# Windowed attention with two gated layers on one core: which engines divide the attention weights, and when the first loads are taken to land

## The chip, the core and the metric

The kernel runs on one core of a Trainium2 chip. The metric is the device time of one execution in microseconds (us), as the median of several runs. The core has TensorE (PE, with its weight loads as PEld), VectorE (DVE), ScalarE (ACT), GpSimd (POOL) and SyncE (SP), which issues most of the loads and stores.

## What is computed

The input is q, k and v for 2 batches of 8 heads, 768 positions and 64 channels. Each position attends to the last 96 positions and to 8 global ones, with a bias that falls with distance. The result, 2 x 768 x 512, goes through two gated layers. All data are float32, the weights of the layers arrive in 64 bits.

```python
scores = scale * q @ k.T + bias            # masked to the window and the global keys
a = np.exp(scores - scores.max(-1))
a = a / (a.sum(-1) + 1e-9)                 # the division that the change moves
x = (a @ v) as 2 x 768 x 512
x = (sigmoid(causal_conv5(x)) * (x @ w_val)) @ w_out
h = relu(x @ w_in2)
out = (h * sigmoid(conv3(h))) @ w_out2
```

The kernel multiplies w_out and w_in2 into one matrix W first, so that the values of the first layer go straight to the hidden units of the second.

## The kernel before

Attention is done in 12 tiles of 128 queries, 6 for each batch (`fast_attention`). A tile needs the keys of itself and of the tile before. For each half of four heads PE writes the scores to PSUM (line 492). DVE adds the bias and takes the extreme of each row (line 503), ACT takes the exponential with its row sum (line 508), POOL adds 1e-9 to four sums (line 519), DVE takes the reciprocals (line 522), and then each of the four heads' weights, the tile `p`, is multiplied by its reciprocal. That last step is called a division here. It is done by DVE (line 529) or by POOL (line 532).

Then, for two heads at a time, PE transposes the weights into the PSUM tile `t` (line 559), ACT or DVE copies them to `pts` (lines 563 and 569), and PE multiplies them with the values into the PSUM tile `x` (line 584). The ring of `t` has a single buffer, so each transposition of two heads waits for the copy of the two before. The tile's result is moved to SBUF on line 601 (ACT) or 607 (DVE).

Meanwhile the weights of the layers are loaded in units of 128 rows and brought from 64 bits to float32 (`to_f32`: lines 272 on ACT, 274 on POOL, 279 and 282 on DVE). PE makes W of them (line 337). The first product of W needs five such units. `hidden_inputs`, `values` (lines 246, 253 to 255, 697, 698, 702, 755) and later `hidden` and `project` follow.

The order on each engine is made when the kernel is built. `Plan.add` takes each step with the engines that can do it and a cost in us for each. `Plan.lay` runs through the steps in a modelled time: the step goes to the engine where it would end first by these costs, from the times in `START` on. Steps of the loads issued ahead (`LANDED`) count as done at the given times. `Plan.issue` then writes every engine's instructions in that order, and each engine keeps to it. A cost or a time in these tables therefore changes no instruction by itself: it changes which engine does a step and where the step stands.

```python
here: ends = {o: max(free[o], est[w]) + us for o, (us, _) in w.ways.items()}
```

Of the kernel before, what the change touches and what calls it, by code (L numbers as in the profile page):

```python
# [13 lines left out]
AF = mybir.ActivationFunctionType  # L14
ALU = mybir.AluOpType
# [24 lines left out]
XPAIRS = 2  # L40
RAWS, MBUFS, HBUFS, Z2BUFS, PBUFS, PTBUFS, KQBUFS, VBUFS = 3, 2, 6, 3, 11, 4, 3, 4
EARLY = -5.0
LANDED = {("k", 1): 2.5, ("k", 2): 3.8, ("r", 1): 5.1, ("v", 1): 6.5, ("r", 2): 7.8}
LANDING = 2.4
ORDERED = {getattr(mybir.EngineType, e) for e in ("PE", "DVE", "Activation", "Pool")}
BANKS = {"s": 4, "t": 1, "x": 1, "f": 2}
# [38 lines left out]
class Plan:  # L85

    LAG = {"PE": 0.2, "ACT": 0.15, "DVE": 0.15, "POOL": 0.15, "SP": 0.0, "AHEAD": 0.0}
    START = {"DVE": 0.4, "ACT": 1.2, "SP": 4.9}  # L90
    SWITCH = 0.1
    STICK = 3.0
    PASSES = 6
# [127 lines left out]
def act_us(n, sbuf=True, scaled=False, sums=False):  # L221
    return 0.05 + 0.000834 * n + 0.042 * sbuf + 0.092 * scaled + 0.093 * sums
# [10 lines left out]
def pool_us(n):  # L233
    return 0.17 + 0.0013 * n
# [201 lines left out]
def fast_attention(c, ap):  # L436

    nc, ident, pl = c.nc, c.ident, c.plan
# [13 lines left out]
    def keys(t, pr, what):  # L452
        return key_tile(t)[:, pr, what]
# [21 lines left out]
    for t in range(nt):  # L475
        b, i = tiles[t]
        if t and i == 0:
            yield
        js = [t - 1, t] if i else [t]
        nk = len(js) * P  # L480
        st, p = sts.new(), {}
        load(t)
        for half in range(2):
            s = [c.ring["s"].new() for z in range(2)]

            def scores(half=half, s=s, js=js, t0=t):
                for pr in (2 * half, 2 * half + 1):
                    for n, j in enumerate(js):
                        for z in range(2):
                            hs = slice(z * D, (z + 1) * D)  # L490
                            out = s[z].t.rearrange("p (a w) -> p a w", w=WIN)[:, pr % 2, n * P : (n + 1) * P]
                            nc.tensor.matmul(out, keys(t0, pr, 1)[hs], keys(j, pr, 0)[hs], start=True, stop=True)  # L492

            pl.add(
                "PE", 0.43 * len(js), scores, s + held(kq, js), [("kq", j) for j in js], [("s", t, half)], mode="s"
            )
            for h in range(4 * half, 4 * half + 4):
                p[h] = pr_.new()

                def least(h=h, s=s, st=st, w=p[h], nk=nk, i=i):  # L500
                    sc = s[h % 2].t.rearrange("p (a w) -> p a w", w=WIN)[:, h // 2 % 2, :nk]
                    bias = c.B[:, h, :] if i else c.B0[h]
                    nc.vector.tensor_tensor_reduce(  # L503
                        w.t[:, :nk], sc, bias, -QKSCALE, 3.0e38, ALU.add, ALU.min, st.t[:, 0, h : h + 1]
                    )

                def grow(h=h, st=st, w=p[h], nk=nk):
                    nc.scalar.activation(  # L508
                        w.t[:, :nk], w.t[:, :nk], AF.Exp, bias=st.t[:, 0, h : h + 1], scale=-1.0,
                        accum_out=st.t[:, 1, h : h + 1],  # L510
                    )

                bias = ("B" if i else "B0", h)
                pl.add("DVE", dve_us(nk), least, [p[h], s[h % 2], st], [("s", t, half), bias], [("p", t, h)])
                pl.add("ACT", act_us(nk, True, True, True), grow, [p[h], st], [], [("p", t, h)])
            hs = slice(4 * half, 4 * half + 4)

            def guard(st=st, hs=hs):
                nc.gpsimd.tensor_scalar(st.t[:, 1, hs], st.t[:, 1, hs], 1.0e-9, 1.0, ALU.add, ALU.mult)

            def invert(st=st, hs=hs):
                nc.vector.reciprocal(st.t[:, 2, hs], st.t[:, 1, hs])  # L522

            four = [("p", t, h) for h in range(4 * half, 4 * half + 4)]
            pl.add("POOL", 0.12, guard, [st], four, [("r", t, half)])
            pl.add("DVE", 0.2, invert, [st], [], [("r", t, half)])
            for h in range(4 * half, 4 * half + 4):
                def on_dve(h=h, st=st, w=p[h], nk=nk):
                    nc.vector.tensor_scalar(w.t[:, :nk], w.t[:, :nk], st.t[:, 2, h : h + 1], None, ALU.mult)  # L529

                def on_pool(h=h, st=st, w=p[h], nk=nk):
                    nc.gpsimd.tensor_scalar(w.t[:, :nk], w.t[:, :nk], st.t[:, 2, h : h + 1], 1.0, ALU.mult, ALU.mult)  # L532

                pl.add(
                    "DVE", 0.13 + 0.00052 * nk, on_dve, [p[h], st], [("r", t, half)], [("p", t, h)],
                    POOL=(0.2 + pool_us(nk), on_pool),
                )

        def first_keys(t=t, i=i):
            r = key_tile(t)[:, :, 0, 0:GW]  # L540
            a, z = (gl, r) if i == 0 else (r, gl)
            nc.gpsimd.tensor_scalar(a, z, 1.0, 1.0, ALU.mult, ALU.mult)

        if i == 0:
            pl.add("POOL", 0.4, first_keys, held(kq, [t]), [("kq", t)], ["gl"])
        elif i < NT - 1:
            pl.add("POOL", 0.4, first_keys, held(kq, [t]), ["gl"], [("kq", t)])

        xp = c.ring["x"].new()
        pts = {}  # L550
        for pr in range(NPAIR):
            pt = c.ring["t"].new()
            pts[pr] = ptr.new()

            def turn(pr=pr, pt=pt, p=p, nw=len(js)):
                o = pt.t.rearrange("p (z n q) -> p z n q", z=2, n=2)
                for z in range(2):
                    for n in range(nw):
                        nc.tensor.transpose(o[:, z, n, :], p[2 * pr + z].t[:, n * P : (n + 1) * P], ident)  # L559

            def copy(pt=pt, w=pts[pr], nw=len(js)):
                o = pt.t.rearrange("p (z n q) -> p z n q", z=2, n=2)
                nc.scalar.activation(w.t[:, :, :nw, :], o[:, :, :nw, :], AF.Copy)  # L563

            two = [p[2 * pr], p[2 * pr + 1]]
            pl.add("PE", 0.218 * len(js), turn, [pt] + two, [("p", t, 2 * pr), ("p", t, 2 * pr + 1)], [("pt", t, pr)])
            def by_dve(pt=pt, w=pts[pr], nw=len(js)):
                o = pt.t.rearrange("p (z n q) -> p z n q", z=2, n=2)
                nc.vector.tensor_copy(w.t[:, :, :nw, :], o[:, :, :nw, :])

            pl.add(
                "ACT", act_us(2 * nk, False), copy, [pt, pts[pr]], [("pt", t, pr)], [("pts", t, pr)],
                DVE=(dve_us(2 * nk), by_dve),
            )

            if pr % XPAIRS < XPAIRS - 1:
                continue

            def output(prs=range(pr - XPAIRS + 1, pr + 1), pts=pts, xp=xp, js=js):
                o = xp.t.rearrange("p (a q) -> p a q", q=P)  # L580
                for pr in prs:
                    for n, j in enumerate(js):
                        for z in range(2):
                            nc.tensor.matmul(  # L584
                                o[z * D : (z + 1) * D, pr, :], vals(j, 2 * pr + z), pts[pr].t[:, z, n, :],
                                start=n == 0, stop=n == len(js) - 1,
                            )

            prs = range(pr - XPAIRS + 1, pr + 1)
            pl.add(  # L590
                "PE", 0.213 * len(js) * XPAIRS, output, [xp] + [pts[q] for q in prs] + held(vs, js),
                [("pts", t, q) for q in prs] + [("v", j) for j in js], [("xp", t, q) for q in prs], mode="x",
            )
        if 0 < i < NT - 1:
            pl.add(
                "SP", dma_us(64), lambda b=b, t=t: nc.sync.dma_start(vs[t].t[0:GW], c.v[b, 0:GW].rearrange("s (a h) d -> s a h d", a=2)),
                [vs[t]], [], [("v", t)], delay=LANDING,
            )
        pl.add(
            "ACT", act_us(512, False),  # L600
            lambda xp=xp, i=i: nc.scalar.activation(
                c.x[:, :, XP + i * P : XP + (i + 1) * P], xp.t.rearrange("p (a q) -> p a q", q=P), AF.Copy
            ),
            [xp], [("xp", t, pr) for pr in range(NPAIR)], [("x", i)] + (["d", "d0"] if t in (0, 1, 4) else []),
            DVE=(
                dve_us(512),
                lambda xp=xp, i=i: nc.vector.tensor_copy(
                    c.x[:, :, XP + i * P : XP + (i + 1) * P], xp.t.rearrange("p (a q) -> p a q", q=P)
                ),
            ),  # L610
        )
# [431 lines left out]
```

## Time and profile before

| | |
|---|---|
| median of 3 runs | 285.67 us (285.6 to 286.19) |
| the profiled execution | 285.83 us |
| its span, from first to last instruction | 284.0 us |
| busy PE | 268.7 us, 95% |
| busy DVE | 235.2 us, 83% |
| busy ACT | 190.2 us, 67% |
| busy POOL | 96.7 us, 34% |

The span is the profiled execution without what lies around it (1.8 us). The shares are means over stages that differ, so the stages have to be read one by one. The time of an instruction in the trace is longer than the distance at which two of them follow each other on an engine, since the end of one lies over the start of the next.

### The profile page before, as it was taken

How to read it: one execution, taken by the hardware profiler on the slowest of the kernel's cores; microseconds unless marked ns; L12 is line 12 of the kernel's file. 1: busy time of each engine (PE TensorE's matmuls, PEld its weight loads, DVE VectorE, ACT ScalarE, POOL GpSimd, SP SyncE). 2: the span in 40 equal slices, each digit the busy share in tenths (PEclk: the TensorE clock that was granted, in tenths of full speed). 3: DMA queues.
4: the chain of work that ended last, by engine and by line, in shares of the span. 5: the costliest groups of instructions: out<-in, count | busy, mean ns of one | idle time of the engine just before them, and what ended most of it. 6: DMA issues, size and time to landing. Idle time of an engine off the chain costs nothing.

```text
span 284.0 us, 5446 instructions
## 1 busy us (share of the span) xinstructions
PE 268.7 (95%) x1832; PEld 227.7 (80%) x1832; DVE 235.2 (83%) x599; ACT 190.2 (67%) x476; POOL 96.7 (34%) x207
## 2 busy tenths in 40 slices
PE   3979999999989989999999999999999999999993
PEld 2857746555569979999899999989999988899883
DVE  3999999999999999998999999999985554357600
ACT  2999984976798798797877455884474354444520
POOL 4544563662395536622446012130412000003000
PEclk9999999999999999999999999999999999999999
DMA  5995554854480320004400000010000020000121
GB/s 155 358 338 186 219 180 150 291 175 149 148 264 35 121 75 14 35 13 158 150 0 0 2 0 1 8 48 21 37 2 0 0 76 37 37 0 2 40 111 48
DMA packets 10421, 26.18 MB, mean 92 GB/s; under 512 B 1424, under 2 KB 2704, under 8 KB 10384
## 3 DMA queue, kind: packets, MB, share of 16 engines
q1 hardware_dynamic: 9968, 25.22, 26.2%
q10 hardware_dynamic: 416, 0.52, 0.5%
q8 instruction: 16, 0.26, 0.4%
q14 instruction: 21, 0.17, 0.2%
HBM read 22.59 MB, written 3.15 MB: 91 GB/s over the span
## 4 chain that ended last, share of the span: by engine, by line
PE 70%; DVE 21%; ACT 3%; issue 3%; POOL 2%; DVEq 1%; ACTq 0%; POOLq 0%
PE s L254 8%; PE s L255 8%; PE s L253 8%; PE f L255 5%; PE f L254 5%; PE f L253 5%; PE s L492 5%; DVE z L702 4%; PE t L559 4%; PE x L584 4%; DVE p L503 4%; PE f L337 4%; PE t L253 2%; DVE p L529 2%; PE x L255 2%
## 5 line engine op out<-in xcount | busy, mean ns | idle before, releaser
L702 DVE SCALAR_TENSOR_TENSOR z<-h,cw,z 128x384 f32<-128x384 f32 x64 | 39.9, 629 | 12.7 <-ACT z L697 10.9
L508 ACT ACTIVATE p<-p,st 128x256 f32<-128x256 f32 (+1 forms) x96 | 46.1, 483 | 6.4 <-DVE st L503 6.4
L704 ACT ACTIVATE z<-z 128x384 f32<-128x384 f32 (+2 forms) x48 | 25.1, 523 | 25.0 <-DVE z L702 24.6
L254 PE MATMUL s<-w,g 128*128 128x512 f32 (+1 forms) x104 | 39.2, 377 | 0.0
L255 PE MATMUL s<-w,g 128*128 128x512 f32 (+1 forms) x104 | 39.2, 377 | 0.0
L702 DVE SCALAR_TENSOR_TENSOR z<-x,cw,z 128x400 f32<-128x400 f32 (+1 forms) x64 | 39.1, 642 | 0.1
L253 PE MATMUL s<-w,g 128*128 128x512 f32 (+1 forms) x104 | 39.1, 376 | 0.0
L532 POOL TENSOR_SCALAR p<-p,st 128x256 f32<-128x256 f32 (+1 forms) x48 | 32.4, 683 | 11.3 <-DVE st L522 6.9
L559 PE MATMUL t<-ident,p 128*128 128x128 f32 x176 | 28.6, 281 | 5.6 <-ACT pts L563 3.4
L559 PEld LDWEIGHTS t<-ident,p 128*128 128x128 f32 x176 | 19.8, 141 | 15.6 <-ACT pts L563 5.9
L503 DVE CUSTOM_DVE_ANT_0 p<-s,B 128x256 f32<-128x256 f32 x80 | 30.8, 412 | 0.3 <-PE s L492 0.3
L337 PE MATMUL f<-w,w 128*128 128x512 f32 x64 | 29.8, 597 | 0.1
L253 PE MATMUL f<-gg,Wh 128*128 128x400 f32 (+1 forms) x80 | 27.7, 346 | 0.0
L255 PE MATMUL f<-gg,Wl 128*128 128x400 f32 (+1 forms) x80 | 27.0, 338 | 0.0
L254 PE MATMUL f<-gg,Wh 128*128 128x400 f32 (+1 forms) x80 | 27.0, 338 | 0.0
L563 ACT ACTIVATE pts<-t 128x512 f32<-128x512 f32 (+1 forms) x40 | 22.1, 552 | 5.7 <-PE t L559 3.7
L274 POOL TENSOR_SCALAR raw<-raw 128x512 f32<-128x512 f32 x24 | 18.1, 754 | 19.8 <-ACT m L272 12.5
L698 POOL TENSOR_SCALAR z<-h,cw 128x384 f32<-128x384 f32 x9 | 8.3, 923 | 44.5 <-DVE z L702 31.0
L246 DVE TENSOR_TENSOR g<-z,g 128x384 fp32r<-128x384 f32 x32 | 17.9, 567 | 5.9 <-ACT g L244 5.9
L255 PEld LDWEIGHTS s<-w,g 128*128 128x128 f32 x104 | 19.5, 188 | 3.9
L254 PEld LDWEIGHTS s<-w,g 128*128 128x128 f32 x104 | 19.5, 188 | 2.8
L253 PEld LDWEIGHTS s<-w,g 128*128 128x128 f32 x104 | 19.5, 188 | 2.8
(125 smaller groups left out, 657.3 us busy)
## 6 DMA issues: line engine op xcount, KB each, us to landing
raw<-in_moe_w_out_dram SPq DMA_DIRECT2D x12, 512.0 KB, 3.5
raw<-in_moe_w_in_dram SPq DMA_DIRECT2D x8, 512.0 KB, 5.2
k<-in_kq_dram SPq DMA_DIRECT2D x7, 512.0 KB, 4.9
v<-in_v_dram SPq DMA_DIRECT2D x11, 256.0 KB, 4.1
out_dram<-o SPq DMA_DIRECT2D x11, 256.0 KB, 2.0
raw<-in_moe_w_val_dram SPq DMA_DIRECT2D x4, 512.0 KB, 3.6
kq<-in_kq_dram SPq DMA_DIRECT2D x3, 512.0 KB, 4.7
v<-in_v_dram SPq DMA_DIRECT2D x8, 64.0 KB, 2.8
```

Source lines behind the costliest of these rows:

```text
L253: nc.tensor.matmul(out, lh, rh, start=first, stop=False)
L254: nc.tensor.matmul(out, lh, rl, start=False, stop=False)
L255: nc.tensor.matmul(out, ll, rh, start=False, stop=last)
L274: "POOL", pool_us(n), lambda: nc.gpsimd.tensor_scalar(whole(), whole(), 0.0, 1.0, ALU.mult, ALU.mult),
L337: nc.tensor.matmul(ps.t, big["wot"].t.bitcast(F32)[:, e, cs], big[wi].t.bitcast(F32)[:, e, :], start=e == 0, stop=e == 3)
L503: nc.vector.tensor_tensor_reduce(w.t[:, :nk], sc, bias, -QKSCALE, 3.0e38, ALU.add, ALU.min, st.t[:, 0, h : h + 1])
L508: nc.scalar.activation(w.t[:, :nk], w.t[:, :nk], AF.Exp, bias=st.t[:, 0, h : h + 1], scale=-1.0, accum_out=st.t[:, 1, h : h + 1],)
L532: nc.gpsimd.tensor_scalar(w.t[:, :nk], w.t[:, :nk], st.t[:, 2, h : h + 1], 1.0, ALU.mult, ALU.mult)
L559: nc.tensor.transpose(o[:, z, n, :], p[2 * pr + z].t[:, n * P : (n + 1) * P], ident)
L563: nc.scalar.activation(w.t[:, :, :nw, :], o[:, :, :nw, :], AF.Copy)
L702: nc.vector.scalar_tensor_tensor(z(), src(k), w()[:, k : k + 1], z(), ALU.mult, ALU.add)
L704: pl.add("ACT", act_us(n), lambda: nc.scalar.activation(z(), z(), AF.Tanh, scale=0.5), bufs, [], [token])
```

## The change

The division's second way is an ACTIVATE with the reciprocals as its scale on ACT, in place of a TENSOR_SCALAR on POOL. The modelled cost on DVE for 256 columns goes from 0.26 to 0.35. The modelled landings of five early loads and the time from which SP is free are later by 0.5 to 1.4 us. Nothing else is edited; the order on all engines is worked out anew.

```diff
-LANDED = {("k", 1): 2.5, ("k", 2): 3.8, ("r", 1): 5.1, ("v", 1): 6.5, ("r", 2): 7.8}
+LANDED = {("k", 1): 3.0, ("k", 2): 5.0, ("r", 1): 6.3, ("v", 1): 7.7, ("r", 2): 9.0}
...
-    START = {"DVE": 0.4, "ACT": 1.2, "SP": 4.9}
+    START = {"DVE": 0.4, "ACT": 1.2, "SP": 6.3}
...
-                def on_pool(h=h, st=st, w=p[h], nk=nk):
-                    nc.gpsimd.tensor_scalar(w.t[:, :nk], w.t[:, :nk], st.t[:, 2, h : h + 1], 1.0, ALU.mult, ALU.mult)
+                def on_act(h=h, st=st, w=p[h], nk=nk):
+                    nc.scalar.activation(w.t[:, :nk], w.t[:, :nk], AF.Copy, scale=st.t[:, 2, h : h + 1])
 
                 pl.add(
-                    "DVE", 0.13 + 0.00052 * nk, on_dve, [p[h], st], [("r", t, half)], [("p", t, h)],
-                    POOL=(0.2 + pool_us(nk), on_pool),
+                    "DVE", 0.22 + 0.00052 * nk, on_dve, [p[h], st], [("r", t, half)], [("p", t, h)],
+                    ACT=(act_us(nk, True, True), on_act),
                 )
```

Of the 96 divisions DVE has 48 and POOL 48 before; with the change DVE has 49, ACT 47 and POOL none. Of the 48 copies to `pts` DVE has 8 before and 14 with the change. ACT has two masks before (line 400) and one with the change, DVE three (line 401, 256 columns) and one, POOL three (line 399) and six.

The first place is PE at the start, after the scores of tile 1 (`k_71` and `k_72` are the keys of tiles 1 and 2); one piece of the difference:

```order
 L492 MATMUL s<-k_71 128x128 x2
-L559 MATMUL t<-ident,p 128x128 x4
-L492 MATMUL s<-k_71,k_72 128x128 x2
-L492 MATMUL s<-k_72 128x128 x2
-L492 MATMUL s<-k_71,k_72 128x128 x2
-L492 MATMUL s<-k_72 128x128 x2
-L559 MATMUL t<-ident,p 128x128 x2
-L584 MATMUL x<-pts,x 64x128 x4
 L559 MATMUL t<-ident,p 128x128 x6
 L584 MATMUL x<-pts,x 64x128 x4
```

The scores of tile 2 stood between the transpositions of tile 0; now three transpositions of tile 0 and a product with the values come first.

The second place is ACT ahead of the first product of W. Before (the transpositions that PE does last ahead of that product wait for the copy `pts_700<-t_682`):

```order
L508 ACTIVATE p_598,st_512<-p_598,st_512 128x256
L508 ACTIVATE p_612,st_512<-p_612,st_512 128x256
L272 ACTIVATE w8_648<-raw1_75 128x4x128
L508 ACTIVATE p_645,st_646<-p_645,st_646 128x256
L563 ACTIVATE pts_672<-t_651 128x512
L508 ACTIVATE p_656,st_646<-p_656,st_646 128x256
L601 ACTIVATE x_70<-x_617 128x4x128
L563 ACTIVATE pts_700<-t_682 128x512
```

The same place with the change (the transpositions of `p_596` and `p_606` are the last ahead of the product there, and they wait for the copy `pts_688<-t_677`):

```order
L508 ACTIVATE p_606,st_524<-p_606,st_524 128x256
L532 ACTIVATE p_562<-p_562,st_524 128x256
L508 ACTIVATE p_624,st_524<-p_624,st_524 128x256
L532 ACTIVATE p_552<-p_552,st_524 128x256
L508 ACTIVATE p_635,st_524<-p_635,st_524 128x256
L272 ACTIVATE w8_662<-raw1_75 128x4x128
L563 ACTIVATE pts_669<-t_639 128x512
L508 ACTIVATE p_659,st_660<-p_659,st_660 128x256
L532 ACTIVATE p_606<-p_606,st_524 128x256
L563 ACTIVATE pts_688<-t_677 128x512
```

Three divisions now stand among the exponentials and copies of this stretch on ACT. From ACT's first exponential to that copy the engine had 34 exponentials, 11 copies, 5 weight units (and the small `cw`), 3 moves of `x` and 2 masks; now it has 33 exponentials, 14 divisions (11 of 256 columns, 3 of 128), 7 copies, the same 5 units and `cw`, 2 moves and 1 mask. DVE, up to the end of the fifth unit, has 36 bias steps and 5 units both before and now, 16 divisions in place of 21, 7 copies in place of 3, and 1 mask of 256 columns in place of 3.

The third place is PE in the last tile of the first batch. Before:

```order
L492 MATMUL s<-k_72 128x128 x2
L559 MATMUL t<-ident,p 128x128 x2
L584 MATMUL x<-pts,v 64x128 x4
L559 MATMUL t<-ident,p 128x128 x4
L253 MATMUL f<-gx,wvh 128x400
```

And with the change:

```order
L492 MATMUL s<-k_72 128x128 x2
L559 MATMUL t<-ident,p 128x128 x2
L584 MATMUL x<-pts,v 64x128 x4
L253 MATMUL f<-gx,wvh 128x400
L254 MATMUL f<-gx,wvh 128x400
L255 MATMUL f<-gx,wvl 128x400
```

Nine more matmuls of the values follow these three before the next transpositions, which stood right behind the line 584 before.

## Rows read from the trace of the kernel before

**Rows 1.** Stages by windows: us, then busy PE, PEld, DVE, ACT, POOL, PEclk, DMA, GB/s

```profile
6.50:20.00 13.50, 11.44 (x106) 8.91 (x106) 13.22 (x67) 12.42 (x47) 6.89 (x20) 1.00 0.97 345
20.00:35.00 15.00, 13.91 (x174) 11.34 (x175) 14.67 (x54) 14.82 (x47) 7.93 (x16) 1.00 0.59 203
35.00:104.00 69.00, 66.50 (x492) 45.09 (x492) 67.41 (x189) 54.10 (x151) 37.18 (x61) 1.00 0.50 166
104.00:140.00 36.00, 35.90 (x327) 33.40 (x324) 34.56 (x92) 30.49 (x78) 16.29 (x37) 1.00 0.21 64
140.00:279.00 139.00, 139.00 (x732) 127.18 (x731) 102.91 (x191) 76.88 (x155) 25.86 (x62) 1.00 0.07 25
```

**Rows 2.** Waits of PE from 6.5 to 35: us in total, times, longest

```profile
PE t L559 <- ACT pts L563: 1.7, 3, 0.7
PE t L559 <- DVE st L503: 0.7, 1, 0.7
PE t L559 <- DVE p L529: 0.3, 1, 0.3
PE t L559 <- ACT cw L272: 0.3, 1, 0.3
```

**Rows 3.** Waits of PE from 35 to 140

```profile
PE t L559 <- ACT pts L563: 1.7, 2, 1.1
PE t L559 <- DVE pts L569: 0.6, 2, 0.3
```

**Rows 4.** Shares of the chain that ended last, from 80 to 104, by line

```profile
by line: DVE z L702 26.1%; DVE p L503 17.8%; DVE p L529 9.5%; DVE z L755 8.0%; DVE gg L246 6.1%; DVE wvl L246 5.8%; DVE Wl L246 4.9%; DVE gx L246 2.7%; PE s L492 2.7%; PE t L559 2.6%; DVE pts L569 2.6%; DVE raw L279 2.5%; DVE x L607 2.5%; D
```

**Rows 5.** Waits of ACT from 6.5 to 34.5

```profile
ACT p L508 <- DVE st L503: 1.2, 3, 0.5
ACT pts L563 <- PE t L559: 0.3, 1, 0.3
```

**Rows 6.** Groups by line and form: count | busy us, mean ns | idle before, releasers

```profile
L508 ACT ACTIVATE p<-p,st 128x256 f32<-128x256 f32 x80 | 39.8, 501 | 4.5 <-DVE st L503 4.5
L532 POOL TENSOR_SCALAR p<-p,st 128x256 f32<-128x256 f32 x40 | 27.8, 704 | 8.6 <-DVE st L522 4.1 <-PE f L253 1.6 <-PE s L492 1.3
L563 ACT ACTIVATE pts<-t 128x512 f32<-128x512 f32 x33 | 19.5, 591 | 3.9 <-PE t L559 3.5
L529 DVE TENSOR_SCALAR p<-p,st 128x256 f32<-128x256 f32 x40 | 16.2, 437 | 0.0
L508 ACT ACTIVATE p<-p,st 128x128 f32<-128x128 f32 x16 | 6.2, 393 | 1.9 <-DVE st L503 1.9
L569 DVE COPY pts<-t 128x512 f32<-128x512 f32 x7 | 4.8, 687 | 0.4 <-PE t L559 0.3
```

**Rows 7.** Timeline of all engines around the first product of W: start, length

```profile
33.86 0.60 ACT L563 ACTIVATE pts<-t 128x512 f32<-128x512 f32 x1
34.35 0.50 ACT L508 ACTIVATE p<-p,st 128x256 f32<-128x256 f32 x1
34.78 0.66 PE L559 MATMUL t<-ident,p 128*128 128x128 f32 x4
34.84 0.49 ACT L508 ACTIVATE p<-p,st 128x256 f32<-128x256 f32 x1
35.27 1.02 PE L337 MATMUL f<-w,w 128*128 128x512 f32 x2
```

**Rows 8.** Timeline: DVE divisions beside a quiet and beside a busy POOL

```profile
30.96 0.35 DVE L529 TENSOR_SCALAR p<-p,st 128x256 f32<-128x256 f32 x1
32.32 0.92 DVE L529 TENSOR_SCALAR p<-p,st 128x256 f32<-128x256 f32 x2
32.57 1.00 POOL L532 TENSOR_SCALAR p<-p,st 128x256 f32<-128x256 f32 x2
```

**Rows 9.** Timeline of PE at its longest wait of the middle stage

```profile
81.54 0.44 PE L559 MATMUL t<-ident,p 128*128 128x128 f32 x2
81.91 0.66 PE L584 MATMUL x<-pts,v 128*64 128x128 f32 x8
83.69 0.52 PE L559 MATMUL t<-ident,p 128*128 128x128 f32 x3 [1.12 <-ACT pts L563]
```

## Prediction

> **What bounds the kernel now.** I read four views: the stages in windows, the waits of PE, the chain of waits, and the groups with their durations. The windows say first where time can be had at all [rows 1]: from 140 to 279 us PE is busy for all of the 139 us, so nothing there gets shorter, and whatever the change does earlier moves that block as a whole. From 6.5 to 35 us, DVE and ACT are both nearly full (13.22 and 12.42 of 13.5 us, then 14.67 and 14.82 of 15), while POOL is half idle (7.93 of 15). From 35 to 104 us DVE is still full (67.41 of 69), but ACT has 14.9 us to spare and PE loses 2.5. After that PE loses next to nothing.
>
> The waits of PE name the losses: 3.0 us in the first stage, 1.7 of it for ACT's copies to `pts` and 1.0 for results of DVE [rows 2]; 2.3 us from 35 on, for copies again, two by ACT and two by DVE [rows 3]. In the chain from 80 to 104 us almost every piece is DVE's [rows 4], so there ACT's late copies are late because DVE was. So the kernel is bound by PE, with an input that ACT and DVE together can just deliver up to 35 us, and that DVE can barely deliver up to 104. All that can be gained is these 5.3 us of waits; what can be lost has no such limit.
>
> **The price of one division.** On POOL one of 256 columns takes 704 ns, on DVE 437 [rows 6]. On DVE it takes 0.35 us when POOL is quiet, and two take 0.92 us when POOL divides beside them [rows 8], so about 0.09 of the 437 ns is POOL's doing. ACT has no division in this trace. The nearest row is the exponential on the same tile, 501 ns with an extra instruction that reads the row sum [rows 6]; from one to the next it takes 0.49 us [rows 7]. A division has no row sum to read. Two instructions overlap by about 0.1 us (the copy of 591 ns is followed by the next instruction after 0.49 [rows 6, 7]), so 0.41 us is my value, the same as the exponential's own record less that overlap. Its ends are 0.40 and the full 0.49. For 128 columns the same step gives 0.30 from 393 ns [rows 6].
>
> **First stage, 6.5 to 35 us: dearer.** PE starts its first product of W at 35.27, right behind a transposition at 34.78, and that follows ACT's copy of 33.86 [rows 7]. The order shows what ACT does up to that copy. Added: 11 large and 3 small divisions, 11 x 0.41 + 3 x 0.30 = 5.4 us. Gone: three large copies at 0.49, a small one at 0.3, one move of `x` and one exponential at 0.49 each, a mask at 0.3, together 3.1. ACT has 2.3 us more to do before the same transposition. What can absorb it is ACT's idle time there, 1.5 us of waits [rows 5], of which half were for rows that DVE had not finished; I let 0.7 of it go. **+1.6 us.** The low end is 0: DVE's work up to the fifth weight unit is five divisions less (at 0.27 apart) and two masks less, but four copies more at 0.6, so about +0.4, less some 1.5 that its remaining divisions no longer lose to POOL, and ACT alone then decides. The high end is the whole 2.3. All of this counts in full: the products of W that fill PE later cannot start earlier, since their weights need the same engines.
>
> **Middle stage, 35 to 104 us: cheaper.** DVE, which sets this stage, gets 4 large and 2 small copies and a small division more and 2 masks less over the kernel: 4 x 0.6 + 2 x 0.3 + 0.2 - 0.6 = +2.6 us. It loses the collisions, 40 x 0.09 = 3.6 us. Net -1.0. Apart from that the order removes the worst wait by itself: PE stood 1.12 us for a copy because only eight short matmuls lay between two transpositions [rows 9]; now twelve matmuls of 0.18 us stand between them, 2.2 us. Of the 2.3 us of waits [rows 3] I take 1.1 for that place and 0.5 of the rest. **-1.6 us.** The best that can happen is -2.3; at the other end the 30 or so divisions that ACT gets here make copies late elsewhere, and nothing is won, or 0.5 is lost. The cover for them is ACT's 14.9 idle us [rows 1] against 30 x 0.41 = 12.3; it is thin, and if it is gone the price is rival 2.
>
> POOL loses 40 x 0.70 us and its small divisions. That is worth nothing directly: POOL waited for others before its divisions [rows 6]. SP's order shifts by a few loads; nothing waited for SP's early loads in rows 2, so I take the landings as a change of order only, at 0, between -3.0 (all the waits of rows 2) and +0.5. The last stage is 0. DVE's work there is the same and PE has no gap in it.
>
> [...]
>
> **Sum.** +1.6 - 1.6 + 0 = 0 against the profiled execution's own 285.83 us, that is 285.8. The median of the runs is 0.16 lower, so I forecast 285.7 us: no change that a measurement of this kernel can tell (about 0.2%, 0.6 us). Its own range is 284.7 to 286.7.
>
> **Rival 1, faster: DVE was the only brake.** ACT swallows the added 2.3 us in its idle time, since DVE feeds it earlier, and the middle stage gives back all 2.3: 285.7 - 2.3 = 283.4. For it: nearly the whole chain of rows 4 is DVE. Against it: ACT's 14.82 of 15 us before the first product.
>
> **Rival 2, slower: ACT becomes the brake.** In order on ACT, a division that waits for DVE's reciprocal holds up the exponentials and copies queued behind it, and PE's transpositions wait for those, one buffer deep. The start costs the full 2.3 and the middle gives nothing back: 285.7 + 2.3 = 288.0. It decides once ACT has under about 1.5 us of idle left in the middle stage. For it: 12.3 of 14.9 idle us are used. Against it: DVE takes over six copies. [...]
>
> **Rival 3, faster: the landings matter.** If the early order was wrong because loads landed later than modelled, the 3.0 us of waits in rows 2 go, and with ACT's +1.6 the sum is 285.7 - 3.0 + 1.6 = 284.3. Against it: none of those waits is for a load.
>
> **How the numbers follow.** Forecast 0.42, rival 1 0.20, rival 2 0.26, rival 3 0.12. The forecast's own range reaches past 0.6 us on either side, so of its 0.42 I give 0.07 to faster, 0.26 to no change and 0.09 to slower. With rival 1, 0.10 of rival 3 and 0.25 of rival 2, the rest to no change: faster 0.37, same 0.29, slower 0.34. The range takes in the forecast, rival 3 and most of rivals 1 and 2: 283.7 to 287.7.
>
> **What would show it.** In the changed profile the first product of W should start between 36 and 37.5 us, with ACT full before it; an ACT division should take about 0.5 us in the record; DVE's division should fall to about 0.35; PE's waits from 35 to 104 should sum to 0.5 to 1.0 us, and no wait of 1 us should be left there. The forecast is wrong if the product starts at 35.3 or earlier (rival 1 or 3), if PE's waits for copies in the middle stage grow beyond 2 us (rival 2), or if PE shows gaps after 140 us.

## The result, and the profile after

The changed kernel takes 288.79 us (median of 6 runs, 287.22 to 288.99) against 285.83 us of the kernel before in the same comparison (6 runs, 285.6 to 286.19). The ratio is 1.0086, with a 95% interval of 1.0066 to 1.0106: slower, by 3.0 us in medians and 2.5 us by the ratio, and above the range that I gave. Ratios are taken over fast runs, and one run, 292.99 us with the landings only, is left out of them and of its kernel's median because it lies more than 1.5% above the fastest of its kernel. The profiled execution of the change took 288.97 us, with a span of 287.1 us, 3.1 more than before.

Three events of the trace cut those 3.1 us into parts: the first product of W, the last matmul of PE, and the end of the span.

| | before | change | difference |
|---|---|---|---|
| first product of W starts | 35.27 | 37.67 | +2.4 |
| from there to the start of the last matmul | 243.66 | 243.23 | -0.4 |
| from there to the end of the span | 5.1 | 6.2 | +1.1 |

So the loss lies at the two ends of the program. I had priced the start at +1.6, the middle at -1.6, and the end at nothing.

The windows of the changed kernel, with the columns of [rows 1]:

```profile
6.50:20.00 13.50, 11.63 (x97) 9.29 (x96) 11.82 (x58) 11.90 (x47) 6.08 (x16) 0.87 0.98 346
20.00:35.00 15.00, 13.60 (x160) 10.87 (x160) 14.01 (x50) 14.72 (x45) 4.50 (x10) 1.00 0.48 157
35.00:104.00 69.00, 67.38 (x484) 45.21 (x486) 66.93 (x200) 62.17 (x175) 18.73 (x34) 1.00 0.51 168
104.00:140.00 36.00, 36.00 (x320) 33.70 (x319) 34.52 (x96) 32.27 (x90) 11.57 (x29) 1.00 0.20 60
140.00:279.00 139.00, 139.00 (x748) 126.82 (x748) 105.76 (x196) 79.75 (x160) 25.91 (x62) 1.00 0.08 29
```

The middle stages answer to [rows 1] much as intended: POOL falls from 37.18 to 18.73 us, ACT rises from 54.10 to 62.17, and PE is busy 0.9 us longer. The surprise is in the first line. PE is busy slightly longer than before, yet it issued 97 matmuls where it had issued 106, and its granted clock is 0.87 where it was 1.00. Cut into single microseconds, the same view shows where the clock fell:

```profile
14.00:15.00 1.00, 1.00 (x14) 0.83 (x12) 0.92 (x4) 1.00 (x4) 0.83 (x2) 0.66 1.05 426
15.00:16.00 1.00, 1.00 (x12) 1.00 (x12) 1.00 (x5) 1.00 (x5) 0.00 (x0) 0.50 1.00 389
16.00:17.00 1.00, 1.00 (x8) 0.45 (x4) 0.82 (x6) 0.15 (x1) 0.00 (x0) 0.50 1.10 422
17.00:18.00 1.00, 1.00 (x11) 1.00 (x12) 0.94 (x5) 0.89 (x4) 0.00 (x0) 0.63 1.01 395
```

In the two middle rows the granted clock is 0.50. The timeline of PE just ahead of them, in the changed kernel, shows what the engine did before its clock fell:

```profile
10.99 0.44 PE L559 MATMUL t<-ident,p 128*128 128x128 f32 x2
12.04 0.41 PE L559 MATMUL t<-ident,p 128*128 128x128 f32 x2 [0.61 <-DVE pts L569]
13.42 0.44 PE L559 MATMUL t<-ident,p 128*128 128x128 f32 x2 [0.97 <-DVE pts L569]
13.79 0.66 PE L584 MATMUL x<-pts,x 128*64 128x128 f32 x8
14.38 0.80 PE L492 MATMUL s<-k,k 64*128 64x128 f32 x4
```

From 11 to 13.8 us PE has three pairs of transpositions and nothing else, each pair held up by the copy of the one before. The scores of the next tile, which would have filled the gaps, now stand behind them; groups of four score matmuls that take 0.39 us each at a clock of 1.00 (from 17.89 and 18.11) take 0.64 at 0.50 (from 14.96, 15.39 and 15.82). In the six runs of the change two took 287.2 and 287.4 us at a mean clock of 0.998 or more, four took 288.8 to 289.0 at 0.987 to 0.989: the clock does not fall in every execution, and where it does it costs about 1.5 us.

The waits of PE from 6.5 to 35 (first fence, against [rows 2]) and from 35 to 140 (second, against [rows 3]) in the changed kernel:

```profile
PE t L559 <- DVE pts L569: 2.8, 3, 1.2
PE t L559 <- ACT p L508: 0.3, 1, 0.3
```

```profile
PE f L337 <- DVE Wl L246: 1.1, 2, 0.9
PE t L559 <- ACT pts L563: 0.6, 1, 0.6
```

At the start the sum is as before (3.1 for 3.0 us), but nearly all of it is now for copies by DVE. In the middle 2.3 us became 1.7, and the worst wait of [rows 9] is gone.

The groups by line and form that answer to [rows 6]:

```profile
L532 ACT ACTIVATE p<-p,st 128x256 f32<-128x256 f32 x40 | 19.2, 500 | 0.0
L563 ACT ACTIVATE pts<-t 128x512 f32<-128x512 f32 x29 | 17.0, 588 | 2.0 <-PE t L559 1.8
L529 DVE TENSOR_SCALAR p<-p,st 128x256 f32<-128x256 f32 x40 | 15.9, 417 | 0.0
L569 DVE COPY pts<-t 128x512 f32<-128x512 f32 x11 | 7.6, 687 | 1.9 <-PE t L559 1.9
```

ACT's division takes 500 ns, as read from the exponential. DVE's division went from 437 to 417 ns in the mean, not to 350; the part on the prediction takes that mean apart.

The last 1.1 us come behind all of the work. The view of the lines of the program's end (line 1038, engines' sequencers) has in the kernel before:

```profile
L1038 ACTq EVENT_SEMAPHORE  x2: 17/17/17, 283.4 to 283.9; - x2
L1038 DVEq EVENT_SEMAPHORE  x2: 21/21/21, 283.4 to 283.9; - x2
```

and in the changed kernel:

```profile
L1038 ACTq EVENT_SEMAPHORE  x2: 17/17/17, 285.4 to 287.0; - x2
L1038 DVEq EVENT_SEMAPHORE  x2: 21/21/21, 286.8 to 287.0; - x2
```

(name, count, shortest/middle/longest ns, first and last start). ACT and DVE pass their first event of the end together at 283.4 before. In the change ACT passes at 285.4 and DVE at 286.8, 1.4 us later, though DVE's last piece of work had ended at 281.69. The whole core waits for it:

```profile
SPq L1038 <- DVEq L1038: 1.4, 1, 1.4
```

### The profile page after: what moved, and what is told of

Read it like the earlier page. It is cut to its first block, busy times and chain, and to the rows that moved or that the text cites. A ratio compares the mean times of both kernels' runs of the same rounds, so it can differ in the third digit from the quotient of the medians.

```text
span 287.1 us, 5391 instructions
## 1 busy us (share of the span) xinstructions
PE 271.5 (95%) x1832; PEld 229.6 (80%) x1832; DVE 235.4 (82%) x604; ACT 202.3 (70%) x516; POOL 69.1 (24%) x162
## 3 DMA queue, kind: packets, MB, share of 16 engines
HBM read 22.59 MB, written 3.15 MB: 90 GB/s over the span
## 4 chain that ended last, share of the span: by engine, by line
PE 79%; DVE 11%; ACT 5%; issue 2%; DMA 1%; DVEq 0%
PE s L254 8%; PE s L255 8%; PE s L253 8%; PE f L253 8%; PE f L255 7%; PE f L254 7%; PE s L492 7%; PE x L584 5%; PE t L559 5%; PE f L337 4%; ACT p L508 3%; PE t L253 2%; PE x L255 2%; PE t L255 2%; PE x L253 2%; PE t L254 2%
## 5 line engine op out<-in xcount | busy, mean ns | idle before, releaser
L702 DVE SCALAR_TENSOR_TENSOR z<-h,cw,z 128x384 f32<-128x384 f32 x64 | 40.6, 643 | 12.4 <-ACT z L697 10.9
L508 ACT ACTIVATE p<-p,st 128x256 f32<-128x256 f32 (+1 forms) x96 | 46.0, 482 | 2.9 <-DVE st L503 2.8
L337 PE MATMUL f<-w,w 128*128 128x512 f32 x64 | 30.5, 605 | 1.2 <-DVE Wl L246 1.1
L698 POOL TENSOR_SCALAR z<-h,cw 128x384 f32<-128x384 f32 x11 | 11.4, 1035 | 49.7 <-DVE z L702 31.0
L244 ACT ACTIVATE g<-z 128x384 fp32r<-128x384 f32 x32 | 16.4, 519 | 7.9 <-DVE z L815 5.4
L532 ACT ACTIVATE p<-p,st 128x256 f32<-128x256 f32 (+1 forms) x47 | 21.6, 484 | 0.0
```

The source lines that it names most:

```text
L337: nc.tensor.matmul(ps.t, big["wot"].t.bitcast(F32)[:, e, cs], big[wi].t.bitcast(F32)[:, e, :], start=e == 0, stop=e == 3)
L508: nc.scalar.activation(w.t[:, :nk], w.t[:, :nk], AF.Exp, bias=st.t[:, 0, h : h + 1], scale=-1.0, accum_out=st.t[:, 1, h : h + 1],)
L532: nc.scalar.activation(w.t[:, :nk], w.t[:, :nk], AF.Copy, scale=st.t[:, 2, h : h + 1])
L702: nc.vector.scalar_tensor_tensor(z(), src(k), w()[:, k : k + 1], z(), ALU.mult, ALU.add)
```

## Experiments

Theory A after this reading had three parts. The start: later landings in the tables put PE's work in an order that leaves it idle, and its clock falls. The end: the event is late by where DVE's last instructions stand in its program, not by what they do. The divisions themselves are about neutral. The rivals were that ACT's divisions hold up the start, and that the divisions themselves cost in the middle stage. All twelve kernels are compared with runs of the kernel before on the same chip.

| run | us (median) | ratio to before, 95% | first W | last matmul | end of span |
|---|---|---|---|---|---|
| before (profile above) | 285.83 | | 35.3 | 278.9 | 284.0 |
| change (profile above) | 288.79 | 1.0066 to 1.0106 | 37.7 | 280.9 | 287.1 |
| division only | 288.59 | 1.0066 to 1.0142 | 35.2 | 281.0 | 287.1 |
| landings only | 290.98 | 1.0096 to 1.0213 | 43.0 | 285.7 | 291.1 |
| filled gap | 287.81 | 1.0041 to 1.0088 | 36.2 | 279.2 | 285.7 |
| moved end | 288.02 | 1.0045 to 1.0100 | 38.8 | 281.9 | 286.9 |
| before, moved end | 286.93 | 1.0027 to 1.0053 | 35.2 | 278.9 | 285.0 |
| gap and end | 286.57 | 1.0015 to 1.0033 | 36.2 | 279.5 | 284.5 |
| one landing back | 285.64 | 0.9984 to 1.0005 | 35.9 | 278.3 | 284.1 |
| three engines | 285.61 | 0.9984 to 1.0003 | 36.1 | 279.0 | 284.0 |
| one back, moved end | 285.59 | 0.9989 to 1.0012 | 35.9 | 278.4 | 283.6 |
| landings, one back | 290.89 | 1.0128 to 1.0210 | 42.8 | 284.5 | 290.0 |
| division, moved end | 287.67 | 1.0061 to 1.0109 | 34.8 | 280.5 | 285.5 |
| three engines, landings | 286.43 | 1.0018 to 1.0043 | 39.9 | 279.6 | 284.7 |

The first product of W is a landmark only among kernels with the same work ahead of it. By the trace PE has 292 matmuls before it in the kernel before, in the change and in the moved ends of these two, and 301 with the filled gap, of which 9 are the extra ones. It has 288 with one landing back and with three engines, 268 with the division alone, 312 with the landings only, 360 with these and one back, and 348 with three engines and landings.

**The two halves of the change, apart.** Division only:

```diff
-LANDED = {("k", 1): 3.0, ("k", 2): 5.0, ("r", 1): 6.3, ("v", 1): 7.7, ("r", 2): 9.0}
+LANDED = {("k", 1): 2.5, ("k", 2): 3.8, ("r", 1): 5.1, ("v", 1): 6.5, ("r", 2): 7.8}
-    START = {"DVE": 0.4, "ACT": 1.2, "SP": 6.3}
+    START = {"DVE": 0.4, "ACT": 1.2, "SP": 4.9}
```

> The division moved to ScalarE as in the change, the landings and SP's start as before. Theory A (three causes: PE idles early because the scores of tile 2 stand late, and its clock then falls to the lower level; ACT has more to do before the first product of W; VectorE reaches the program's end late): here four transpositions, four products with values and then the scores of tile 2 follow, so PE has less to idle over, the granted clock from 10 to 20 us stays at 1.00 or loses less than 0.05, the first product starts near 36 us and the time is 286.0 to 287.3 us. Theory B (the division on ScalarE is the whole loss, the landings none): the time is that of the change, 288.5 to 289 us. Theory C (the landings are the whole loss): 285.7 us.

Measured: 288.59 us, so the expected 286.0 to 287.3 was missed, and the time is the one that theory B named. The clock is 1.00 up to 140 us. The first product stands at 35.2, no later than before, but the last matmul is 2.0 us late. The windows up to the first product, of the kernel before (first line) and of this one, show where these 2.0 us are lost:

```profile
6.50:35.27 28.77, 25.62 (x280) 20.52 (x279) 28.16 (x122) 27.50 (x94) 14.82 (x35) 1.00 0.77 271
6.50:35.15 28.65, 24.74 (x256) 19.17 (x253) 27.39 (x111) 26.78 (x92) 11.61 (x27) 1.00 0.77 259
```

PE has done 24 matmuls fewer, 16 of scores and 8 transpositions. At the 25.62 us for 280 of the kernel before that is 2.2 us of work (an estimate), which has to be done later. So the start is slower with the division alone, and from the first product on nothing is lost or won: 245.8 us less 2.2 is 243.6, for 243.7 before. The waits that the trace lists for PE carry a part of it. From 6.5 to 35 they are 3.8 us, 0.8 more than before, and those for ACT's copies have doubled from 1.7 to 3.4; from 35 to 140 they are only 1.0, but 0.7 follow after 140. The rest of the 2.2 stands in no listed wait. From 6.5 to 35:

```profile
PE t L559 <- ACT pts L563: 3.4, 5, 1.3
PE x L584 <- ACT x L601: 0.2, 1, 0.2
PE x L584 <- DVE pts L569: 0.2, 1, 0.2
```

And the end is late here too, in a place that tells more. Now DVE's first event of the end is in time, and the DRAIN behind it is late: it stands at 286.7, while ACT's stands at 285.5.

```profile
L1038 DVEq EVENT_SEMAPHORE  x2: 21/21/21, 285.4 to 287.0; - x2
L1038 ACTq DRAIN  x1: 8/8/8, 285.5 to 285.5; - x1
...
L1038 DVEq DRAIN  x1: 129/129/129, 286.7 to 286.7; - x1
```

Landings only (the change's LANDED and START in the kernel before):

> The later landings and SP's start alone, the division on VectorE and GpSimd as before. Theory A: four transpositions of tile 0 come before the scores of tile 2, as in the change, so PE idles between 11 and 14 us, the granted clock from 10 to 20 us falls under 0.9 in most executions, and the time is 286.8 to 287.8 us with the first product of W 1 to 2 us later than in the kernel before. Theory B: 285.7 us, and a first product at 35.3 us. Theory C: 288.5 to 289 us.

Measured: 290.98 us (three runs, 288.40 to 291.84), by the ratio 4.4 us more than before: far more than expected, and in the wrong way for anyone who took the landings for harmless. Its profile is of the longest execution, 292.99 us. There the clock fell twice, and PE lost time to single waits of up to 1.6 us:

```profile
6.50:20.00 13.50, 12.07 (x103) 10.15 (x101) 11.90 (x61) 9.45 (x39) 7.33 (x21) 0.87 0.95 335
20.00:35.00 15.00, 12.61 (x127) 9.76 (x125) 11.39 (x43) 13.20 (x42) 5.34 (x13) 0.91 0.43 138
```

The clock is not all of it: the run of 288.40 us had a mean clock of 1.000 and is still 2.3 us slower than before (286.07 in that comparison).

The ratios of the halves, 1.0104 and 1.0155, do not add up to the change's 1.0086. The halves are not independent: each gives another order on all engines, and the later landings on top of the division cost nothing that the intervals can tell.

**The clock.** Filled gap: nine transpositions of the identity into an unused buffer, three behind the first pair and six behind the second.

```diff
+                for n in range((3, 6)[pr] if fill else 0):
+                    nc.tensor.transpose(fill.t[:, (n % 4) * P : (n % 4 + 1) * P], ident, ident)
```

> The change, with nine transpositions of the identity put on PE behind the first two of tile 0, where it waits for copies; their results are not used, everything else keeps its order. Theory A: with PE at work there its granted clock stays at 1.00 from 10 to 20 us in every execution, the first product of W comes 1.0 to 1.6 us earlier than in the change (at 36.1 to 36.7 us), and the time falls to 287.2 to 287.5 us in all rounds, though PE does more. Rival (the clock is a mere sign, the loss is the wait for copies): the extra 1.4 us of PE work lies in the waits, and the time stays at 288.8 us or grows.

Measured: 287.81 us, with two runs at 287.3 and 287.5 as expected and two at 288.1. More work on PE made the kernel 1.0 us faster than the change (medians; the intervals of the two overlap, and the square below settles it), and its profile has the first product 1.5 us earlier. In the same microseconds as above the clock is now full:

```profile
14.00:15.00 1.00, 1.00 (x18) 0.88 (x16) 1.00 (x5) 1.00 (x6) 0.00 (x0) 1.00 1.04 422
15.00:16.00 1.00, 1.00 (x12) 0.71 (x10) 1.00 (x5) 1.00 (x5) 0.00 (x0) 1.00 1.04 393
16.00:17.00 1.00, 1.00 (x16) 0.88 (x15) 1.00 (x7) 1.00 (x5) 0.27 (x1) 1.00 1.04 412
17.00:18.00 1.00, 1.00 (x13) 0.78 (x12) 0.81 (x5) 1.00 (x6) 0.37 (x2) 1.00 1.03 395
```

So PE's idle time among those transpositions, two gaps of 0.61 and 0.97 us in the change and of 0.51 and 0.56 here, had brought the clock down; how long such a gap must be for it no run here shows. Neither here nor in the run with gap and end below, 15 executions together, is the mean clock under 0.994; in four of the change's six it was 0.989 or less. The first product is still 0.9 us later than before. How much of that is the order, how much ACT's added divisions and how much the nine extra transpositions, the runs do not separate.

**The end.** Moved end: six clears of a small tile by DVE in the arm of the program that is not taken. They are never executed; they only shift the instructions behind them.

```diff
+                pad = c.small.tile([P, 1], F32, name="pad")
+
+                def unused():
+                    for _ in range(6):
+                        nc.vector.memset(pad, 0.0)
+
+                pl.add("DVE", 0.0, unused)
```

> The change, with six small memsets more on VectorE in the arm of the program that is not run, so that only the place of the program's end among VectorE's instructions moves. Theory A: the last event of VectorE comes with the others', within 0.2 us, instead of 1.4 us behind, and the time falls by 1.0 to 1.4 us to 287.4 to 287.8 us. Rival (the late end comes from the last store, or from the late clock): nothing moves, 288.8 us.

Measured: 288.02 us, 0.8 less than the change and above the expected 287.4 to 287.8. This run alone does not show what the end is worth: like the change's, its runs lie at 287.3 to 287.4 and at 288.6 to 289.1 us, with lower mean clocks in both groups (0.990 to 0.994, and 0.983 to 0.987). In the profiled execution the clock had fallen for longer than in the change's (0.75 over 6.5 to 20 us), so the first product was even later, at 38.8; but the span ended 4.2 us after DVE's last work, as before (4.3), and no longer 5.4.

The other way round, nine such clears in the kernel before:

> The kernel before with nine extra clears of a small tile by DVE, in the arm of the program that is not taken, so that DVE's instructions behind the taken arm stand where they stand in the change. Nothing that is executed changes. Theory A (the last 1.1 us of the change are the place of the end of DVE's program, not its schedule): last DVE instruction starts at 279.3 as before (within 0.3), SP's wait at the end for an engine's event grows from 0.6 in all to 1.4 or more, the span to 285.0 to 285.4, the time to 286.7 to 287.2. Rival (the late event comes of what DVE executed in the changed schedule): no difference, 285.7 to 286.1 and a wait of 0.6.

Measured: 286.93 us, 1.2 more than before (285.72 there), with an interval of 1.0027 to 1.0053. The last matmul starts at 278.93 as before, to the hundredth, and the late event is there:

```profile
L1045 ACTq EVENT_SEMAPHORE  x2: 17/17/17, 283.4 to 285.0; - x2
L1045 DVEq EVENT_SEMAPHORE  x2: 21/21/21, 284.7 to 285.0; - x2
```

Instructions that are never executed cost 1.2 us. The number of DVE's instructions in the built programs orders all the cases. The end has three instructions on DVE that matter: an event, a drain, an event. With 2120 in all (the change, filled gap, before with moved end) the first of them is late by 1.3 to 1.4 us; with 2119 (division only) the second, by 1.2; with 2118 (one landing back, below) the third, by 0.85; with 2093 to 2116 (before, landings only, three engines) and with 2126 (the moved ends) none. In each case it is the instruction at one and the same place, third from the end of 2120 or last of 2118, and what stands there is late, whatever it is. Why that place is slow no run here shows.

**Both at once.** The filled gap together with the moved end:

> The change with both suspected costs removed at once: nine transpositions of the identity into an unused buffer in PE's gap at 11 to 14 us (their product is not read), and six unused clears that move the end of DVE's program. Theory A (clock and end are all that the change lost, against a middle stage that it won): first product of W at 36.2, granted clock 1.00 from 6.5 to 20, end 4.2 to 4.4 after the last DVE instruction, so 285.7 less 1.1 to 1.4 of span: time 286.0 to 286.7, the same as before (285.8 to 286.1). Rival B (something is lost in the middle stage too): 287 or more with the end in order. Rival C (the change is a gain of its own once these are removed): under 285.5.

Measured: 286.57 us (11 runs), inside the expected 286.0 to 286.7. The four kernels make a square: 288.79 us without either, 287.81 with the gap filled, 288.02 with the end moved, 286.57 with both. So the gap is worth 1.0 to 1.45 us and the end 0.8 to 1.2, and the interval of the run with both, 1.0015 to 1.0033, lies below those of the runs with one, which begin at 1.0041 and 1.0045. Of the change's 3.0 us, 2.2 are gone and 0.85 are left. The profiled execution (286.24 us) has the start 0.9 late, and the middle gives 0.4 back: from the first product to the last matmul 243.3 us for 243.7.

**Which landing.** One landing back: the change with a single number of the table restored.

```diff
-LANDED = {("k", 1): 3.0, ("k", 2): 5.0, ("r", 1): 6.3, ("v", 1): 7.7, ("r", 2): 9.0}
+LANDED = {("k", 1): 3.0, ("k", 2): 3.8, ("r", 1): 6.3, ("v", 1): 7.7, ("r", 2): 9.0}
```

> The change with one of its five landings put back, that of tile 2's keys (3.8 for 5.0); PE's order then has tile 1's scores after the first four transpositions again, not after six and a product. Theory A (the later landings' order in the first 20 us is what left PE idle and brought its clock down): granted clock 1.00 from 6.5 to 20 and first product of W at 35.2 to 36.3, against 37.67; time 285.8 to 287.5, by whether the end is late. Rival (ScalarE's divisions hold up the start, whichever order): clock below 1.00, first product after 37, time 288 to 289.

Measured: 285.64 us, the same as before (0.9984 to 1.0005). The timeline of PE at the same place:

```profile
11.87 0.44 PE L559 MATMUL t<-ident,p 128*128 128x128 f32 x2 [0.47 <-DVE st L503]
12.23 0.49 PE L492 MATMUL s<-k,k 64*128 64x128 f32 x4
12.56 0.39 PE L492 MATMUL s<-k 64*128 64x128 f32 x4
12.78 0.39 PE L492 MATMUL s<-k,k 64*128 64x128 f32 x4
13.01 0.39 PE L492 MATMUL s<-k 64*128 64x128 f32 x4
13.32 0.44 PE L559 MATMUL t<-ident,p 128*128 128x128 f32 x2
```

The scores stand between the transpositions again, and no wait is left at 13.3. PE waits for nothing that the trace lists from 35 to 140, though once for 1.0 us after it, and the stretch from the first product to the last matmul is 242.4 us, 1.3 less than before. With this one number the rest of the change keeps what it was to win in the middle, and spends at the start 0.6 us and the four transpositions that it has not done by then.

Landings only, with the same number restored:

> The landings of the change alone (divisions on GpSimd and VectorE as before), with tile 2's keys put back to 3.8; the landings alone cost 5.6 us. Theory A (that one landing does the harm, by the order of the first 20 us): granted clock 1.00 from 6.5 to 35 and time 285.3 to 287.3. Rival (the later landings together do it, or landings and divisions must fit each other): clock below 1.00 again or first product of W after 38, time 288 to 292.

Measured: 290.89 us (ratio 1.0169), no better than without it (1.0155). The rival holds: that one landing is not harmful by itself. It is the order that came out of these landings together with these divisions, and another table gives another one.

**Could one beat both?** The kernel with one landing back had DVE's very last event 0.85 us late, so I moved its end too (eight clears):

> The change with tile 2's keys landing put back (as in the run of one landing back) and eight unused clears that move the end of DVE's program; there DVE's very last event came 0.85 late, which is what the clears should take away. Theory A (the place of DVE's end costs whatever the schedule): end 4.2 to 4.4 after the last DVE instruction for 5.0, so 285.64 less 0.6 to 0.9, time 284.7 to 285.1, faster than the kernel before by 0.2 to 0.35%. Rival (that late event was hidden, or the clears bring another late end): 285.5 to 286.

Measured: 285.59 us, a miss. The span fell by 0.5 us to 283.6, as it should, but the time did not: in these two kernels the time of a run does not contain the wait for DVE's very last event. A late first or second instruction of the end does hold up the others, and does count: 1.2 us in the kernel before with its end moved (286.93 us), 0.9 with the division alone (288.59 us, and 287.67 with its end moved, below).

The division alone with its end moved:

> The division alone, with seven unused clears that move the end of DVE's program; there DVE's last drain came 1.3 late. Theory A: end 4.2 to 4.4 after the last DVE instruction, time 288.6 less 1.0 to 1.3, so 287.2 to 287.6; the 2 us by which its last matmul is late stay, since they lie in the order of the middle stage. Rival (those 2 us belong to that execution, not to the order): 286 or less.

Measured: 287.67 us, 0.9 less than without and just above the expected range. First product (34.8) and last matmul (280.5) repeat those of the division alone within half a microsecond. PE again has 268 matmuls ahead of the first product. So the 2 us are of its order and no accident of one execution; they lie at the start, not in the middle as I had expected.

Three engines: GpSimd's way is kept and ACT's is added, with the landings of before.

```diff
+                    ACT=(act_us(nk, True, True), on_act),
                     POOL=(0.2 + pool_us(nk), on_pool),
```

> The kernel before, its landings included, in which a division may go to ScalarE too, so to any of VectorE, ScalarE and GpSimd, with the price of VectorE that the change has (0.22). Theory A (GpSimd was not what made VectorE's divisions dear, and its time was free): no worse than before in the middle stage, 285.0 to 287.0, by whether the end is late. Rival (GpSimd's divisions cost through the transfers of waits that they cause, which the change removed): PE waits from 35 to 142 of 2.3 us as before, and time no better than 286. If the order alone decides, anything from 285 to 288.5.

Measured: 285.61 us, no difference from before. POOL did 28 of the large divisions, ACT 28, DVE 24. The waits of PE from 38 to 142 fell to 0.6 us; those at the start were 4.1. And the same with the change's landings, tile 2's keys at 3.8:

> The change with GpSimd allowed as a third engine for a division, and tile 2's keys landing put back. Theory A (all three engines give the schedule the most room; the end of DVE's program lies as in the run with three engines and the old landings, where it was not late): 284.5 to 285.8. Rival (PE's order in the first 35 us decides more than where divisions run; here six transpositions stand ahead of tile 1's scores, as in the change): clock below 1.00, 287 to 289.

Measured: 286.43 us, between the two expectations: the clock stayed at 1.00, against the rival, but the time is 0.8 above before. None of the twelve is faster than the kernel before.

## Why the prediction was wrong

I had forecast 285.7 us and no change. By its own steps:

- **The landings "as a change of order only, at 0".** This is the step that failed first. The reason given, that nothing waited for SP's early loads, is true and beside the point: the loads did not move the time, the order did. In the change's order PE stood idle among three pairs of transpositions, its clock fell to 0.87 over 6.5 to 20 us, and 1.5 us of the start's 2.4 came of that. With one number of the table restored the clock stayed at 1.00, the last matmul came 2.6 us earlier, and the time fell by 3.15 us (288.79 to 285.64), a part of it at the program's end. My range for the term was -3.0 to +0.5; alone, the landings cost 4.4 by the ratio. But no order has a price of its own: without any of the new landings the division alone was as slow as the change. I had looked at what the order changed around places where PE waited before, and not at what it did to PE's first 20 us, where the scores of tile 2 no longer filled the gaps.
- **First stage, +1.6 by ACT's added work.** It measured +2.4, and the prediction had no term for the clock, since [rows 1] show 1.00 in every stage. Beside the clock 0.9 is left, below the 1.6. With the division alone PE was 2.2 us of work behind at the first product, and its waits for ACT's copies had doubled. That is inside my range of 0 to 2.3, so the mechanism of this term is borne out there, while in the change PE's waits at the start were for DVE's copies.
- **Middle stage, -1.6.** It measured -0.4. The kind of gain was right: the 1.12 us wait of [rows 9] went, and the chain from 80 to 104, nearly all DVE in [rows 4], is all PE in the change. What was wrong is that no new waits would come: PE now waits 1.1 us for DVE's pieces `Wl` of the weights (line 246) ahead of products of W, and its waits from 35 to 104 sum to 1.7 us where I had written 0.5 to 1.0. With one landing back -1.3 came, close to the forecast.
- **DVE's division to 0.35 us.** The two prices were read rightly. Before, the 10 of the 40 divisions of 256 columns with nothing on POOL beside them take 341 ns in the mean, and the 19 with a division on POOL for more than half of their time take 490. What failed is the step from there to 0.35 for all. POOL kept its other work, and in the change 14 divisions met it and took 549 ns in the mean, while 26 beside a quiet POOL took 346. So the mean fell only to 417 ns, and the term of 3.6 us was 40 x 0.02 = 0.8. One of the 14, beside a weight unit on POOL:

```profile
30.97 0.70 POOL L274 TENSOR_SCALAR raw<-raw 128x512 f32<-128x512 f32 x1 [1.19 <-ACT w L272]
31.00 0.82 DVE L529 TENSOR_SCALAR p<-p,st 128x256 f32<-128x256 f32 x1
```

  From these means the 40 divisions lost 40 x (437 - 341) ns = 3.9 us before, an estimate close to the 3.6 that I had. Why a division on DVE takes longer beside a busy POOL was not shown.
- **The last stage at 0.** PE's part of it was 0. Behind it lay 1.1 us that no view of the work can show, since they depend on how many instructions DVE's program has.
- **The rivals.** Rival 2 has the right side and nearly the time (288.0). For the change that is luck: ACT had 6.8 us left from 35 to 104, the waits at the start were for DVE's copies, and the clock and the end made up the time. The division alone is closer to it, since its start cost 2.2 us and nothing came back; with its end moved it took 287.67 us. But there too ACT had 6.0 us left in the middle. Rival 3 said that the landings matter, with the sign reversed. Rival 1 did not come either.

In medians, with the gap filled first and the end moved then, the 3.0 us are: about 1.0 for the clock (1.5 in the executions in which it falls), 1.2 for the end, and 0.85 for what is left of the start less the middle's gain; that is 3.05. By the ratios the three are 0.6, 1.2 and 0.7.

## What to carry to other kernels

Where a table of times sets the order of work, an edit of the table is an edit of every queue: read the new order of the engine that bounds the kernel from its first instruction on, and look above all for stretches in which it now has only work that waits for one small buffer. In this kernel idle time of TensorE near the start, 0.61 and 0.97 us, was paid for twice, once as idle time and once by its clock, 0.50 from 15 to 17 us. When you cut a time difference at a landmark, count the work ahead of it: the first product of W came no later with the division alone, but with 24 matmuls fewer done. And compare two kernels only after looking at what comes behind the last instruction of work: here 1.2 us hung on the number of instructions in one engine's program.

## What the runs showed of the chip that was not expected

- The granted clock of TensorE fell from 1.00 to 0.50 after two gaps of 0.61 and 0.97 us among three pairs of transpositions, and not in every execution of the same kernel: the mean clock was 0.998 or more in two of six and 0.989 or less in four. Both gaps are waits for the copy out of the one PSUM buffer for the transpositions; a second buffer was not tried. With nine useless transpositions there it stayed at 1.00 from 14 to 18 us.
- The instruction at one place near the end of DVE's program came 0.85 to 1.4 us late, in every profile of a kernel that had one of the end's instructions there.
- The span of a profile and the time of a run are not the same measure at the end: 0.5 us of span, at DVE's very last event, were no time at all.
- A division on DVE took 341 ns in the mean beside an idle POOL and 490 beside a division on POOL, and up to 825 ns beside other work of POOL.
